# First q blocks ahead of the units, smaller first loads, and VectorE and store orders from summed TensorE times, in a two-problem attention block

## The chip, the cores and the metric

One core of one Trainium2 chip. The metric is the device time of one execution in microseconds (us). Before the change: 745.29 us, the median of three runs (745.06 to 746.17).

In what follows a run is called fast or slow by its own kernel: slow is more than 1.5% above that kernel's fastest run. "Span" is the length of the one execution that the profile shows; it is some 1.7 us shorter than the time of the same execution (738.26 us timed, 736.5 us span).

## The reference

Two independent problems, A and B, of the same shapes; the outputs are concatenated on the last axis. All tensors are bf16.

```python
B, Sq, D = 16, 80, 576
Hq, Hkv, Sk, Dh = 32, 16, 512, 128
# x (16,80,576)  k_cache, v_cache (16,16,512,128)  wq (576,4096)  wo (4096,576)
def block(x, k_cache, v_cache, wq, wo):
    q = (x @ wq).reshape(B, Sq, Hq, Dh).transpose(0, 2, 1, 3)
    k = jnp.repeat(k_cache, 2, axis=1)
    v = jnp.repeat(v_cache, 2, axis=1)
    p = softmax(jnp.einsum("bhqd,bhkd->bhqk", q, k) * Dh ** -0.5)
    o = jnp.einsum("bhqk,bhkd->bhqd", p, v)
    return o.transpose(0, 2, 1, 3).reshape(B, Sq, Hq * Dh) @ wo
out = jnp.concatenate([block(A...), block(B...)], axis=-1)
```

## The kernel before

The kernel is written as a list of operations, each with an engine and a number, its key. Each engine runs its operations in the order of their keys, and the semaphore waits are derived from what each reads and writes. So the order of an engine is set by keys alone, and most of the change is a change of keys.

The work is cut in 128 **units** (one batch, four K/V heads: 0.52 MB of K, loaded with a DMA transpose from SyncE's queue, and 0.52 MB of V from ScalarE's queue). A unit has 16 keys. For each four units there are eight **q blocks** (five matmuls), for each eight units ten **output groups** (eight matmuls with wo). There are five K buffers, three V input buffers, three q buffers and two output slots. q blocks, transposes and output groups are "jobs", which take turns in three PSUM banks; a job therefore waits until the one three before it has been drained, that is, until VectorE or ScalarE has copied or added its result out of the bank. The drain of an output group goes to a running sum, `acc`; that of a problem's last quarter adds the sum and goes to `osb`, an output slot, from where it is stored.

```python
NK, NV, NVP, NQ, NOSB, NWARM = 5, 3, 5, 3, 2, 10     # (one line here)
...
def add(eng, key, emit, **kw):
    return S.add(eng, key + 1000.0, emit, **kw)
...
# loads of x, of the first weights, of wo
t = (-800.0, -785.5, -776.5, -771.0)[c] if prob == 0 else 16.0 * (48 + 4 * c) + 9.0
add("sp", t, em_ldx, ...)
add("sp", t + 0.1, em_ldx2, ...)
...
for hf in range(2):                    # first wq in two halves of 512 columns
    add("act", -799.0 + hf, em_a, ...)
    add("act", -798.9 + hf, em_b, ...)
...
t = 256.0 * goct - 56.0 + 22.0 * pc
add("sp", t if goct else 4.0 + 12.0 * pc, em_wo, ...)
...
# q blocks: m counts groups of four units, i the eight blocks of each
t = 64.0 * m - 88.0 + 8.0 * i + 3.3
if m == 0:
    t = -96.0 + 2.0 * i
if m == 1:
    t = -28.0 + 8.0 * i + 3.3
job(t, em_qp, ..., [(ev, t + 2.3, em_qev, ...)])          # drain: 2.3 keys later
...
# K and V of unit U
t_k = T0 - 16.0 * (NK - 1) - LA + 1.5 if U >= NK else -790.0 + 4.5 * U
t_v = (T0 - 16.0 * NV - 8.0) if U >= NV else -780.0 + 3 * U
...
# reciprocal and normalisation (DVE) of a block of P.V results
tn = tmain(W, 3 * f + 2) + 0.8 if f < 5 else 64.0 * W + T_PR + 3.4 + 0.5 * (f - 5)
add("dve", tn, em_rcp, ...)
add("dve", tn + 0.1, em_nrm, ...)
...
# transposes of the normalised result, drained one key later
t = (tmain(W, 3 * lastf + 2) if lastf < 5 else 64.0 * W + T_PR + 4.0) + 5.5 + (1.0 if u == 4 else 0.0)
job(t, em_tr, ..., [("dve", t + 1.0, em_tev, ...)])
...
# output groups and their drain; stores
t = 128.0 * h8 + 64.0 + 12.8 * n + 1.3
job(t, em_op, rd, "op%d.%d" % (h8, n), ..., [("dve", t + 3.4, em_ev, ...)])
add(se, t + 6.0 + 0.1 * pi, em_st, ...)
```

## Time and profile before

| | |
|---|---|
| time, median of 3 | 745.29 us |
| span of the profiled execution | 736.5 us |
| TensorE matmuls / weight loads, share of the span | 93% / 79% |
| VectorE, ScalarE | 53%, 52% |
| all DMA | 160.8 MB, 218 GB/s over the span |

Two things stand between the 659 us of TensorE work and the span: a start in which four loads stop TensorE in turn, and a thin, regular loss afterwards where a job waits for VectorE, an engine that is half idle. The prediction shows both in the profile's own lines.

### The profile page before, as it was taken

How to read it: one execution, taken by the hardware profiler on the slowest of the kernel's cores; microseconds unless marked ns; L12 is line 12 of the kernel's file. 1: busy time of each engine (PE TensorE's matmuls, PEld its weight loads, DVE VectorE, ACT ScalarE, POOL GpSimd, SP SyncE). 2: the span in 40 equal slices, each digit the busy share in tenths (PEclk: the TensorE clock that was granted, in tenths of full speed). 3: DMA queues.
4: the chain of work that ended last, by engine and by line, in shares of the span. 5: the costliest groups of instructions: out<-in, count | busy, mean ns of one | idle time of the engine just before them, and what ended most of it. 6: DMA issues, size and time to landing. Idle time of an engine off the chain costs nothing.

```text
span 736.5 us, 21197 instructions
## 1 busy us (share of the span) xinstructions
PE 688.4 (93%) x9355; PEld 580.9 (79%) x9355; DVE 393.9 (53%) x986; ACT 379.9 (52%) x728; POOL 241.8 (33%) x136
## 2 busy tenths in 40 slices
PE   6827999999999999999999999999999999999995
PEld 3726888888888888888888888888888888888883
DVE  1322554565666555656655554555566566556654
ACT  1513655655555555455555656655555555555560
POOL 4141332244433224443323444332344432234430
PEclk9987999999999999999999999999999999999998
DMA  9999899999999999999999999999899989999841
GB/s 243 159 264 211 188 207 240 247 239 197 221 231 237 215 197 235 216 270 228 235 266 269 241 233 194 273 219 234 200 222 244 239 201 196 242 214 211 205 109 38
DMA packets 365332, 160.79 MB, mean 218 GB/s; under 512 B 283760, under 2 KB 361200, under 8 KB 365232
## 3 DMA queue, kind: packets, MB, share of 16 engines
q1 hardware_dynamic: 296304, 90.98, 67.5%
q10 hardware_dynamic: 68928, 68.37, 30.4%
q8 instruction: 75, 1.23, 0.7%
q14 instruction: 25, 0.20, 0.1%
HBM read 85.98 MB, written 2.95 MB: 121 GB/s over the span
## 4 chain that ended last, share of the span: by engine, by line
PE 82%; DVE 7%; SPq 4%; DMA 4%; issue 1%; ACT 1%
PE ps L788 23%; PE ps L972 21%; PE ps L815 15%; PE ps L880 13%; PE ps L937 6%; PE ps L896 5%; DMA kT<-in_A_k_cache_dram 3%; DVE o_sb L919 3%; SPq L847 2%; DVE oM L944 1%; DVE qT L795 1%; SPq L725 1%; DVE rinv L914 1%; DVE acc L989 1%; DMA wo_sb<-in_A_wo_dram 1%
## 5 line engine op out<-in xcount | busy, mean ns | idle before, releaser
L820 ACT ACTIVATE P<-ps 128x480 bf16<-128x480 f32 (+1 forms) x683 | 366.7, 571 | 322.5 <-PE ps L815 320.1
L854 POOL COPY v_sb<-v_in 128x2048 bf16<-128x2048 bf16 x128 | 239.2, 1896 | 469.9 <-PE ps L896 357.4
L815 PE MATMUL ps<-qT,kT 128*128 128x160 bf16 x2048 | 247.8, 233 | 8.2 <-DMA kT<-in_A_k_cache_dram 8.2
L788 PE MATMUL ps<-xT,wq_sb 128*128 128x320 bf16 x1280 | 218.6, 303 | 12.7 <-DVE acc L989 4.1
L880 PE MATMUL ps<-v_sb,P 128*128 128x130 bf16 x2048 | 203.8, 221 | 0.0
L795 DVE CAST qT<-ps 128x320 bf16<-128x320 f32 x252 | 130.4, 518 | 127.8 <-PE ps L788 127.6
L815 PEld LDWEIGHTS ps<-qT,kT 128*128 128x128 bf16 x2048 | 159.4, 98 | 25.0 <-issue 8.7
L788 PEld LDWEIGHTS ps<-xT,wq_sb 128*128 128x128 bf16 x1280 | 117.8, 99 | 52.7 <-issue 7.9
L972 PE MATMUL ps<-wo_sb,oM 128*128 128x288 bf16 x1024 | 147.1, 287 | 10.3 <-DMA wo_sb<-in_A_wo_dram 10.0
L880 PEld LDWEIGHTS ps<-v_sb,P 128*128 128x128 bf16 x2048 | 149.0, 98 | 8.7
L919 DVE TENSOR_TENSOR o_sb<-ps,rinv 128x384 bf16<-128x384 f32 (+1 forms) x224 | 120.5, 538 | 7.7
L972 PEld LDWEIGHTS ps<-wo_sb,oM 128*128 128x128 bf16 x1024 | 96.6, 98 | 31.0 <-DMA wo_sb<-in_A_wo_dram 10.3
L944 DVE COPY oM<-ps 128x512 bf16<-128x512 bf16 x128 | 54.3, 425 | 70.2 <-PE ps L937 62.0
L914 DVE RECIPROCAL rinv<-ps 128x3 f32<-128x3 f32 (+1 forms) x224 | 39.4, 176 | 94.8 <-PE ps L880 69.6
L937 PE MATMUL ps<-ident,o_sb 128*128 128x128 bf16 x640 | 62.5, 220 | 7.2 <-DVE o_sb L919 7.1
L937 PEld LDWEIGHTS ps<-ident,o_sb 128*128 128x128 bf16 x640 | 43.6, 98 | 16.1 <-DVE o_sb L919 13.7
L989 DVE TENSOR_TENSOR acc<-ps,acc 128x288 f32<-128x288 f32 x80 | 36.2, 452 | 20.6 <-PE ps L972 20.6
L896 PE MATMUL ps<-v_sb,P 128*32 128x130 bf16 x2048 | 36.4, 223 | 0.6 <-DVE o_sb L919 0.6
L972 PE MATMUL ps<-wo_sb,oR 128*128 128x288 bf16 x256 | 36.4, 286 | 0.0
L896 PEld LDWEIGHTS ps<-v_sb,P 128*32 128x32 bf16 x2048 | 30.6, 97 | 4.9 <-DVE o_sb L919 1.0
L972 PEld LDWEIGHTS ps<-wo_sb,oR 128*128 128x128 bf16 x256 | 24.3, 98 | 5.6
L994 DVE TENSOR_TENSOR osb<-ps,acc 128x288 bf16<-128x288 f32 x40 | 18.1, 453 | 10.0 <-PE ps L972 9.9
(22 smaller groups left out, 43.6 us busy)
## 6 DMA issues: line engine op xcount, KB each, us to landing
v_in<-in_A_v_cache_dram ACTq DMA_DIRECT2D x64, 512.0 KB, 5.0
v_in<-in_B_v_cache_dram ACTq DMA_DIRECT2D x64, 512.0 KB, 5.2
wo_sb<-in_A_wo_dram SPq DMA_DIRECT2D x16, 288.0 KB, 4.8
wo_sb<-in_B_wo_dram SPq DMA_DIRECT2D x16, 288.0 KB, 4.8
wq_sb<-in_B_wq_dram SPq DMA_DIRECT2D x16, 256.0 KB, 4.8
wq_sb<-in_A_wq_dram SPq DMA_DIRECT2D x12, 256.0 KB, 5.1
out_dram<-osb SPq DMA_DIRECT2D x32, 72.0 KB, 4.1
wq_sb<-in_A_wq_dram ACTq DMA_DIRECT2D x2, 512.0 KB, 5.1
```

The costliest lines, as they stand in the source:

```text
L788: last = e.matmul(ps[:, bank, 0:QN], lhsT=wq_sb[:, wsl, ck, i * 128:(i + 1) * 128], rhs=xT[:, xsl, ck, :], start=(ck == 0), stop=(ck == 4))
L795: return e.copy(dst, src) if ev == "act" else e.tensor_copy(dst, src)
L815: last = e.matmul(ps[:, sbk, c * 160:(c + 1) * 160], lhsT=kT[:, U % NK, j, g * 128:(g + 1) * 128], rhs=qT[:, (U // 4) % NQ, U % 4, g, :], ...
L820: return e.activation(P[:, psl, 0:k, :], ps[:, sbk, 0:k * 160].rearrange("p (c n) -> p c n", c=k), AF.Exp, scale=SCALE)
L854: return e.tensor_copy(v_sb[:, vps, :, 0:128], v_in[:, vs, :, :].rearrange("p g (j d) -> p (g j) d", j=4))
L880: last = e.matmul(ps[:, bank, off:off + OP_], lhsT=pap(16 * U + 4 * g + j, 0, 128), rhs=v_sb[:, vps, 4 * g + j, :], start=(j == 0), stop=( ...
L896: last = e.matmul(ps[32 * g:32 * g + 32, bank, off:off + OP_], lhsT=pap(16 * U + 4 * g + j, 128, 160), rhs=v_sb[:, U % NVP, 4 * g + j, :], ...
L914: return e.reciprocal(rinv[:, c0:c0 + nt], ps[:, bank, 128:128 + OP_ * (nt - 1) + 1:OP_])
L919: return e.tensor_tensor(o_sb[:, osl, 0:nt, :], src, sc, AluOpType.mult)
L937: last = e.transpose(psb[:, bank, 128 * n_:128 * n_ + 128], o_sb[:, F % NOF, pos, :], ident[:])
L944: return e.tensor_copy(oM[:, osl2, :, 128 * b8:128 * b8 + 128], psb[:, bank, 0:512].rearrange("p (g c) -> p g c", g=4))
L972: last = e.matmul(ps[:, bank, 0:DC], lhsT=w, rhs=wo_sb[:, wsl, i, ch * DC:(ch + 1) * DC], start=(i == 0), stop=(i == 7))
```

## The change

The intent is in three parts.

1. **Start.** Sixteen q blocks, which need only x and wq, are put ahead of the units, to fill the time in which K and V arrive; the third and fourth sets of q blocks come earlier too. The first loads are reordered (x and K interleaved, V later) and the first wq comes in smaller pieces. The first output groups and their weights come later.
2. **VectorE and store order.** The sums of TensorE's modelled durations give the moment at which each TensorE operation should end. Every drain, reciprocal and normalisation is given the key just after its source's end, a store one 1.2 us later. Transposes are put two to four keys later.
3. **End.** The last output tile, which goes out in eight stores of 16 rows, changes places with the full tile before it, so that the last stores are two of 64 rows for each half of the columns.

```diff
-        t = (-800.0, -785.5, -776.5, -771.0)[c] if prob == 0 else ...      # x
+        t = (-800.0, -799.0, -797.0, -794.0)[c] if prob == 0 else ...
-            for hf in range(2):                                            # first wq
-                n0, n1 = hf * 512, (hf + 1) * 512
+            add("act", -799.5, em_b, ...)               # its last 64 rows, in one load
+            for hf, (n0, n1) in enumerate(((0, 256), (256, 512), (512, 1024))):
-            add("sp", t if goct else 4.0 + 12.0 * pc, em_wo, ...)
+            add("sp", t if goct else 58.0 + 13.0 * pc, em_wo, ...)
-                t = -28.0 + 8.0 * i + 3.3                                  # q, m == 1
+                t = -44.0 + 3.5 * i
+            if m == 2:
+                t = -6.0 + 7.0 * i + 3.3
+            if m == 3:
+                t = 54.0 + 8.0 * i + 3.3
-        t_k = ... if U >= NK else -790.0 + 4.5 * U
+        t_k = ... if U >= NK else (-798.0, -796.0, -795.0, -793.0, -792.0)[U]
-        t_v = (T0 - 16.0 * NV - 8.0) if U >= NV else -780.0 + 3 * U
+        t_v = (T0 - 16.0 * NV - (8.0 if U > 8 else -6.0)) if U >= NV else (-84.0, -60.0, -40.0)[U]
...
+    def place_followers():                       # part 2
+        seq = sorted(pe_time, key=lambda x: (x[0].key, x[0].seq))
+        start, end, keys, t = [], {}, [], 0.0
+        for op, d in seq:
+            start.append(t); t += d; end[id(op)] = t; keys.append(op.key)
+        ...
+        for op, (src, sub, lag) in follow:
+            r = end[id(src)] + lag
+            i = bisect.bisect_left(start, r - 1e-6)
+            op.key = keys[i - 1] + (keys[i] - keys[i - 1]) * min(0.999, 0.5 + sub)
+    # durations: scores 0.2076, P.V 0.228, remainder 1.12, q 0.68, output 0.98, transposes 0.228
-            add("dve", tn, em_rcp, ...)
+            add("dve", 0.0, em_rcp, ..., after=(tn, sub, 0.0))
-            t = ... + 5.5 + (1.0 if u == 4 else 0.0)                       # transposes
+            t = ... + (9.5 if u < 3 else 7.5) + (1.5 if u == 4 else 0.0)
-            add(eng, ek, ..., name="ev_" + name)                           # drains
+            add(eng, 0.0, ..., name="ev_" + name, after=(jo, 0.35, 0.0))
-            t = 128.0 * h8 + 64.0 + 12.8 * n + 1.3                         # output groups
+            t = (128.0 * h8 + 66.0 + 12.8 * n if h8 else 112.0 + 12.8 * n) + 1.3
...
+            if h8 == NH8 - 1 and ti > 2:         # part 3
+                ti = 7 - ti
+            last = h8 == NH8 - 1 and n >= 8      # its stores: one for each half of the columns
```

(Cut: the loads of the second wq block, 60 keys later, and the alternation of the last stores over two queues.)

## The prediction

> **What bounds the kernel now.** I read the page first: engine shares and the slices.
>
> ```profile
> PE 688.4 (93%) x9355; PEld 580.9 (79%) x9355; DVE 393.9 (53%) x986; ACT 379.9 (52%) x728; POOL 241.8 (33%) x136
> ...
> PE   6827999999999999999999999999999999999995
> ...
> PEclk9987999999999999999999999999999999999998
> DMA  9999899999999999999999999999899989999841
> ```
>
> TensorE is the densest engine from the fifth slice on (a slice is 18.4 us); the first four slices and the last are holed. The DMA row is at 9 nearly all along, so loads are the second suspect, most of all where TensorE is holed. Since busy matmuls overlap, I took the cost of TensorE's work from its timeline, start to start of consecutive groups where nothing was waited for: a q block (5 matmuls, L788) 0.68 us, 3 score matmuls (L815) 0.208, a P·V group of 4 (L880) 0.23, the 64 remainder matmuls (L896) 1.06, 4 transposes (L937) 0.22, an output group of 8 (L972) 0.975. With 256, 683, 512, 32, 160 and 160 of them: 174 + 142 + 118 + 34 + 35 + 156 = 659 us. The span is 736.5, so about 77 us are not work. Where they lie, by the timeline: 9.7 before the first real matmul, 27 lost between 9.7 and 62 us, about 32 spread thinly over 62 to 728.6, and 7.9 after the last matmul.
>
> The early loss, in the list of waits:
>
> ```profile
> PE ps L972 <- DMA wo_sb<-in_A_wo_dram: 10.0, 1, 10.0
> ...
> PE ps L815 <- DMA kT<-in_A_k_cache_dram: 8.2, 3, 5.1
> ...
> PE ps L788 <- DMA xT<-in_A_x_dram: 2.8, 1, 2.8
> ```
>
> and in the timeline (start, length, engine, line, operation, in brackets idle time before):
>
> ```profile
> 9.69 7.78 PE L788 MATMUL ps<-xT,wq_sb 128*128 128x320 bf16 x40 [3.91 <-issue]
> 20.30 2.19 PE L788 MATMUL ps<-xT,wq_sb 128*128 128x320 bf16 x10 [2.84 <-DMA xT<-in_A_x_dram]
> ...
> 39.62 0.37 PE L815 MATMUL ps<-qT,kT 128*128 128x160 bf16 x3 [2.88 <-DMA kT<-in_A_k_cache_dram]
> ...
> 49.29 0.56 PE L815 MATMUL ps<-qT,kT 128*128 128x160 bf16 x3 [5.12 <-DMA kT<-in_A_k_cache_dram]
> ...
> 59.85 2.10 PE L972 MATMUL ps<-wo_sb,oM 128*128 128x288 bf16 x8 [10.00 <-DMA wo_sb<-in_A_wo_dram]
> ```
>
> TensorE is stopped by four loads in turn. The worst is an output projection put so early that its weights, queued behind K loads, aren't there: with K5 landed, scores and P·V behind it stand still too. From 62 us on there is no load wait on TensorE; the thin loss is this:
>
> ```profile
> PE ps L937 <- DVE o_sb L919: 7.1, 32, 0.3
> ...
> PE ps L788 <- DVE acc L989: 4.1, 16, 0.4
> ...
> PE ps L788 <- DVE osb L994: 1.6, 6, 0.4
> ```
>
> One case of it in the timeline:
>
> ```profile
> 395.44 0.42 DVE L944 COPY oM<-ps 128x512 bf16<-128x512 bf16 x1 [1.76 <-PE ps L937]
> ...
> 396.19 0.44 DVE L994 TENSOR_TENSOR osb<-ps,acc 128x288 bf16<-128x288 f32 x1
> ...
> 396.69 0.85 PE L788 MATMUL ps<-xT,wq_sb 128*128 128x320 bf16 x5 [0.40 <-DVE osb L994]
> ```
>
> VectorE sat idle 1.76 us for a transpose, while the output group begun at 393.16 (done by 394.1) waited to be drained behind it in program order. Its bank came free at 396.63, and the q block that wanted the bank stopped. VectorE is only 53% busy: it is its order that is wrong. Such a stop costs more than the listed idle: start to start the score group before this q block took 0.77 instead of 0.21, 0.56 lost for 0.40 listed.
>
> **What the Trainium skill says.** "Perfetto Trace Analysis", Identifying the Most-Contended Engine: busy share of matmuls is no good measure of headroom, weight-load share is better. Agrees: PE shows 93%, weight loads 79%, my 659 us of work is 89% of the span. "DMA: Bandwidth & Descriptors", Anatomy of one DMA: waiting for a semaphore is done by the issuing sequencer, before dispatch. So one blocked K load holds every later load of SP's list; the trace has SP waiting 542 us in all for TensorE to free K buffers. Same page, Queues, rings and completion order: each DMA engine shares itself round-robin among the queues that have work. Agrees: K3 to K5, issued while V loads ran on the other queue, took 11.0, 13.6 and 12.4 us to land, 6.2 at the median in steady state. "TensorE: Matmul & The Clock Gate", What's actually happening: after an idle window of about 3.4 us TensorE runs at half clock. The windows view has clock 0.50 from 50 to 64 us; a q block there took 1.33 instead of 0.68.
>
> **The change part by part.**
>
> (1) First loads. SP's list becomes x0, x1, K0, x2, K1, K2, x3, K3... and V0 to V2 leave ACT only after the first casts; the first weights come as 256, 256, 512 columns. Now the first q block waited for the tail of x0, issued at 2.24, landing 7.4 later (9.64), with three V blocks (1.5 MB) and K0 in flight beside it. Without those I expect it at about 7 us: 2.5 earlier.
>
> (2) Order of TensorE. The new program shows 80 q matmuls (16 blocks) ahead of the first score, then scores with the third and fourth q blocks' work (m=2, 3) a unit or more earlier than before. 16 x 0.68 = 10.9 us of work that needs x and weights alone, from 7 to 18 us, just while K and V arrive. The output groups of the first eight units start 48 keys (three units) later, their weights too. So the waits of 2.8 and 10.0 us go, with the half clock after them. But K is then the limit. Landings now: K0 15.7, K1 19.8, K2 23.5, K3 33.4, K4 39.5, K5 49.1, with x3 and eight V loads among them. The same bytes in the new order, at that pace: K0 at 14, K2 24, K4 38, K5 44, then some 5 us for each unit (0.52 MB of K, as much of V and part of a weight block, at 230 to 250 GB/s): K8 at 59, K11 at 75. TensorE needs only 3.9 us per unit there (1.1 scores, 0.9 P·V, 0.27 remainder, 0.28 transposes, 1.36 q), so it still waits, about a microsecond a unit. At U11.6 both programs have all 32 early q blocks done; the old one stands there at 97 us with 9 output groups, the new one at some 79 with 5. 97 - 79 - 4 x 0.98 = 14 us gained. (2.5 of part 1 is inside this.)
>
> (3) VectorE order. Each drain, reciprocal and normalisation is now placed where the summed durations of TensorE say its source ends, and transposes come 2 to 4 keys later (4 keys are 1.3 us), so that normalisation has ended. Nothing is added: same instructions. Loss from 62 to 728 by kind of step, start to start: scores before q block 10.2, scores before transpose 8.0, P·V before transpose 4.7, transpose before output 0.8: 23.7 us. I take two thirds as recovered: 16.
>
> (4) End. Stores of the last tile: now eight of 18 KB, issued by two sequencers in 2.5 us after the last addition (729.4); span end 736.5. The last tile becomes one with two stores of 36 KB, halves stored apart: 2 us saved.
>
> Sum: 745.3 - 14 - 16 - 2 = 713; rounded to 712.
>
> **Rivals.** (a) DMA becomes the bound. All 160.8 MB, at 736.5 us a mean of 218 GB/s; a unit of 5.39 us (100 units from 154.5 to 693.3) would become 5.23, which needs 240. If loads can't do that, K never regains its lead and parts 2 and 3 shrink together: some 725 to 730. For it: the DMA row at 9, and 24 us at only about 208 GB/s while TensorE starved (26 to 50). Against it: 251 GB/s held from 350 to 400 with no wait on TensorE, and K landing 6.2 us after issue with 20 us until use. (b) The start is bound by bytes, not order: what the 16 blocks fill is then waited for at K4 to K8 again, and only the 10 us of wo and its half clock remain; with part 3 at 16, about 717. (c) The modelled times are off (clock, load waits), the waits move to other pairs: part 3 gives 5, total 723. (d) Everything works, with VectorE waits nearly gone and K at 4.5 us a unit: 702.
>
> **Range and chances.** Two savings of similar size and different cause, either alone giving about 2%, so a miss of both is needed to stay within 2% (730.4 or more). I predict 712, with 701 (d) to 727 (a with half of part 3) as the range. Faster by over 2%: 0.90; within: 0.09; slower: 0.01, since no work is added.
>
> **What would show it.** First q block at 7, not 9.7; no wait on wo before 110 us; clock near 1 from 10 to 70 us; a few load waits on K of 1 to 3 us left between 25 and 75; U11.6 reached near 79. Waits of L937's and L788's successors on VectorE under 4 us together from 100 to 700, and 5.22 to 5.27 us per unit there. Between last matmul and end about 6 us. I am wrong if K waits run on past 100 us (a), or if the unit time stays at 5.35 or more (c).

## More of the kernel before

One more view of this kernel is needed to compare with later: the table of windows (start:end, length, then busy time of TensorE, its weight loads, VectorE, ScalarE and GpSimd, then granted clock, DMA share, GB/s).

```profile
0.00:50.00 50.00, 33.44 (x326) 23.30 (x326) 13.75 (x33) 16.78 (x32) 16.74 (x16) 0.95 1.09 216
50.00:70.00 20.00, 10.15 (x87) 8.29 (x88) 2.96 (x7) 4.58 (x10) 1.80 (x2) 0.62 0.99 214
```

Loads move at about 215 GB/s in both, while TensorE is idle a third and a half of the time.

## The result and the profile after

| | before | after |
|---|---|---|
| median of the runs taken together (fast) | 745.17 us | 718.64 us |
| range of these (4 runs each) | 736.97 to 746.17 | 712.77 to 719.86 |
| profiled execution, span | 736.5 us | 711.0 us |

Ratio 0.9654, with an interval of 0.9581 to 0.9727: faster. (A ratio here is the mean time of one kernel's fast runs over that of the other's of the same rounds, so not quite the ratio of the medians quoted.) Of six runs of the changed kernel, a slow one, 725.79 us, is left out; a fifth fast one is at 718.41. Both results are correct.

The shares and slices of the changed kernel (a slice is 17.8 us):

```profile
PE 678.5 (95%) x9355; PEld 581.9 (82%) x9355; DVE 388.7 (55%) x986; ACT 377.4 (53%) x728; POOL 241.5 (34%) x136
...
PE   6992999999999999999998999999999999999994
...
PEclk8996999999999999999999999999999999999998
DMA  9999999999999999999999999999899988999921
```

The second and third slices are now full, but the fourth, at 53 to 71 us, is nearly empty. The list of waits (engine, line, what was waited for: total us, times, longest) says why. Lines have moved: output groups are L1007, q blocks L817, scores L844, transposes L970, drains into the output slots L1029.

```profile
PE ps L1007 <- DMA wo_sb<-in_A_wo_dram: 14.0, 1, 14.0
...
DVE osb L1029 <- DMA out_dram<-osb: 7.4, 3, 4.9
...
PE ps L817 <- DMA xT<-in_A_x_dram: 4.3, 1, 4.3
...
PE ps L1007 <- DVE oR L984: 2.1, 1, 2.1
...
PE ps L970 <- DVE o_sb L951: 0.7, 2, 0.6
```

Against the list of before: the 32 transposes that waited for VectorE are 2, and the 16 q blocks that waited for `acc` are gone; the three waits for K are gone. The wait for wo is still there, and longer: 14.0 instead of 10.0. In TensorE's timeline:

```profile
9.87 13.77 PE L817 MATMUL ps<-xT,wq_sb 128*128 128x320 bf16 x80 [4.29 <-DMA xT<-in_A_x_dram]
...
52.61 0.84 PE L817 MATMUL ps<-xT,wq_sb 128*128 128x320 bf16 x5
...
67.46 2.08 PE L1007 MATMUL ps<-wo_sb,oM 128*128 128x288 bf16 x8 [14.01 <-DMA wo_sb<-in_A_wo_dram]
```

The 16 q blocks run back to back, the units run on without a stop until 53.4, then the first output group stands for 14 us before its weights. SyncE's queue, which issues them, shows what they stood behind (start, length of the issue):

```profile
52.89 7.96 SPq L877 DMA_TRANSPOSE kT<-in_A_k_cache_dram  x1
60.89 0.58 SPq L789 DMA_DIRECT2D wo_sb<-in_A_wo_dram  x1
...
62.02 0.43 SPq L789 DMA_DIRECT2D wo_sb<-in_A_wo_dram  x1
```

The group needs all four pieces of wo. Two were issued at 45.07 and 51.76; the other two came behind the load of K10, whose issue alone lasted 7.96 us (2.4 at the median between 100 and 650 us). Only 0.6 of it is listed as a wait for a K buffer. The windows, to be read beside those of before:

```profile
0.00:50.00 50.00, 44.11 (x466) 33.30 (x467) 22.20 (x53) 22.93 (x43) 17.58 (x16) 0.93 1.10 246
50.00:70.00 20.00, 5.99 (x58) 4.64 (x56) 2.47 (x6) 3.03 (x6) 1.89 (x1) 0.66 1.14 231
```

TensorE is busy 10.7 us more in the first 50 us. Loads move 246 GB/s instead of 216, but in the second pair of profiles it is 229 after and 232 before, so that rate is not shown to be the change's doing. From 50 to 70 TensorE does less than before, while loads go on at 231 GB/s. So the DMA engines aren't idle in the gap; they carry something else than wo first.

**Where the time went, by stage.** I took from TensorE's timeline when the first scores of units 12, 22 and 122 start (the first group of three score matmuls that lies wholly in the unit), of two profiled executions of each kernel (the second pair is from the repeat runs b2 and a2 below).

| | unit 12 | unit 22 | 22 to 122 | 122 to the end | span |
|---|---|---|---|---|---|
| before | 99.7 | 154.5 | 538.8 | 43.2 | 736.5 |
| before again | 95.8 | 150.6 | 545.1 | 45.5 | 741.2 |
| after | 86.0 | 142.9 | 523.3 | 44.8 | 711.0 |
| after again | 90.5 | 147.4 | 529.4 | 43.6 | 720.4 |

On the means: up to unit 22, 7.4 us saved; the 100 units between, 15.6; the end, 0.1. Together 23.1 of the span. At unit 12 the kernel before has nine output groups behind it and the changed kernel six; three groups at 0.98 us are 2.9, so of the 9.5 us there some 6.6 are real.

### The profile page after: what moved, and what is told of

It is laid out like the page before. It is cut to its first block, busy times and chain, and to the rows that moved or that the text cites. A ratio compares the mean times of both kernels' runs of the same rounds, so it can differ in the third digit from the quotient of the medians.

```text
span 711.0 us, 21206 instructions
## 1 busy us (share of the span) xinstructions
PE 678.5 (95%) x9355; PEld 581.9 (82%) x9355; DVE 388.7 (55%) x986; ACT 377.4 (53%) x728; POOL 241.5 (34%) x136
## 4 chain that ended last, share of the span: by engine, by line
PE 93%; DMA 2%; SPq 1%; DVE 1%; issue 0%; ACT 0%; DVEq 0%
PE ps L817 25%; PE ps L1007 22%; PE ps L844 20%; PE ps L911 17%; PE ps L970 5%; PE ps L927 5%; SPq L877 1%; DMA xT<-in_A_x_dram 1%; DMA wo_sb<-in_A_wo_dram 1%; DMA out_dram<-osb 1%; DVE o_sb L951 0%; DVE oM L977 0%; DVE osb L1029 0%; SPq L752 0%; DVE okm L1067 0%
## 5 line engine op out<-in xcount | busy, mean ns | idle before, releaser
L849 ACT ACTIVATE P<-ps 128x480 bf16<-128x480 f32 (+1 forms) x683 | 360.5, 570 | 252.7 <-PE ps L844 247.8
L844 PE MATMUL ps<-qT,kT 128*128 128x160 bf16 x2048 | 244.3, 233 | 0.2 <-ACT P L849 0.2
L817 PE MATMUL ps<-xT,wq_sb 128*128 128x320 bf16 x1280 | 215.8, 302 | 5.9 <-DMA xT<-in_A_x_dram 4.3
L844 PEld LDWEIGHTS ps<-qT,kT 128*128 128x128 bf16 x2048 | 159.8, 97 | 18.1 <-ACT P L849 0.4
L1007 PE MATMUL ps<-wo_sb,oM 128*128 128x288 bf16 x1024 | 147.6, 288 | 14.0 <-DMA wo_sb<-in_A_wo_dram 14.0
L817 PEld LDWEIGHTS ps<-xT,wq_sb 128*128 128x128 bf16 x1280 | 117.7, 98 | 39.0 <-issue 5.0
L1007 PEld LDWEIGHTS ps<-wo_sb,oM 128*128 128x128 bf16 x1024 | 97.8, 98 | 38.0 <-issue 14.3
L970 PE MATMUL ps<-ident,o_sb 128*128 128x128 bf16 x640 | 60.0, 219 | 0.8 <-DVE o_sb L951 0.7
L970 PEld LDWEIGHTS ps<-ident,o_sb 128*128 128x128 bf16 x640 | 44.4, 98 | 3.3 <-DVE o_sb L951 1.5
L1007 PE MATMUL ps<-wo_sb,oR 128*128 128x288 bf16 x256 | 38.6, 297 | 2.1 <-DVE oR L984 2.1
L1019 ACT COPY acc<-ps 128x288 f32<-128x288 f32 x40 | 15.9, 398 | 45.2 <-PE ps L1007 45.2
L1029 DVE TENSOR_TENSOR osb<-ps,acc 128x288 bf16<-128x288 f32 x40 | 18.3, 457 | 33.0 <-PE ps L1007 23.5
```

The source lines that it names most:

```text
L817: last = e.matmul(ps[:, bank, 0:QN], lhsT=wq_sb[:, wsl, ck, i * 128:(i + 1) * 128], rhs=xT[:, xsl, ck, :], start=(ck == 0), stop=(ck == 4))
L844: last = e.matmul(ps[:, sbk, c * 160:(c + 1) * 160], lhsT=kT[:, U % NK, j, g * 128:(g + 1) * 128], rhs=qT[:, (U // 4) % NQ, U % 4, g, :], ...
L849: return e.activation(P[:, psl, 0:k, :], ps[:, sbk, 0:k * 160].rearrange("p (c n) -> p c n", c=k), AF.Exp, scale=SCALE)
L970: last = e.transpose(psb[:, bank, 128 * n_:128 * n_ + 128], o_sb[:, F % NOF, pos, :], ident[:])
L1007: last = e.matmul(ps[:, bank, 0:DC], lhsT=w, rhs=wo_sb[:, wsl, i, ch * DC:(ch + 1) * DC], start=(i == 0), stop=(i == 7))
```

## The experiments

Line numbers differ a little from kernel to kernel. All edits are to the changed kernel, unless it says otherwise. Experiments of one job share a chip and its runs of the kernel before: medians of those are 742.57 (first job: e1 to e4), 744.31 (second: a2, b2, e5, e7) and 745.63 (third: e6, e8, e9), slow runs included. Where a view is a span, it is one execution.

### e1: the start alone

VectorE's order, the transposes' and output groups' places, the stores' keys and the end back to the old ones; loads, q blocks and the later first output groups kept.

```diff
-            add(eng, 0.0, ..., name="ev_" + name, after=(jo, 0.35, 0.0))
+            add(eng, ek, ..., name="ev_" + name)
-            add("dve", 0.0, em_rcp, ..., after=(tn, sub, 0.0))
+            add("dve", tn, em_rcp, ...)              # the same for em_nrm, old tn
-            ... + (9.5 if u < 3 else 7.5) + (1.5 if u == 4 else 0.0)
+            ... + 5.5 + (1.0 if u == 4 else 0.0)
-                ti = 7 - ti                          # and last = False
```

> The changed kernel with VectorE order, transpose and store places and the end put back to those of before; only the start (first loads, q blocks ahead, first output groups later) is new. If gains add up by part (my theory): 10 to 13 us faster than before, about 733 to 735 where before is 745, unit time from the 22nd to the 122nd unit back at 5.39 us. If DMA is the bound of the whole kernel (rival a): the start's gain is eaten later by waits on K, under 5 us remain.

Measured: median 737.53 us, ratio to the kernel before 0.9977 (0.9908 to 1.0046); span 732.5, unit 12 at 86.8, units 22 to 122 in 543.0. The old waits are back in its list, at nearly their old size:

```profile
PE ps L970 <- DVE o_sb L951: 7.3, 33, 0.3
...
PE ps L817 <- DVE acc L1022: 4.1, 16, 0.4
```

The start alone brings little to the time, less than the 10 to 13 us expected, and it does nothing for the units after it: 543.0 is the pace of before (538.8 and 545.1).

### e2: VectorE's order alone

The old loads, q places and end; part 2 kept.

```diff
-        t = (-800.0, -799.0, -797.0, -794.0)[c] if prob == 0 else ...
+        t = (-800.0, -785.5, -776.5, -771.0)[c] if prob == 0 else ...
-            add("sp", t if goct else 58.0 + 13.0 * pc, em_wo, ...)
+            add("sp", t if goct else 4.0 + 12.0 * pc, em_wo, ...)
         # likewise wq, K, V, the q blocks and the first output groups: old keys; old end
```

> The kernel before with only VectorE's order taken from modelled TensorE times, later transposes, and store places; old start, old end. Additive theory: 15 to 18 us faster than before (about 728 to 730), unit time 5.23 us, start as before with the 10 us wait on the output weights. Rival (VectorE's order matters only once TensorE is ahead of loads, or DMA binds): under 8 us.

Measured: median 728.15 us, ratio 0.9835 (0.9761 to 0.9909); span 718.6, units 22 to 122 in 531.2. In its list:

```profile
DVE osb L1025 <- DMA out_dram<-osb: 18.1, 4, 6.2
...
PE ps L1003 <- DMA wo_sb<-in_A_wo_dram: 10.7, 1, 10.7
...
PE ps L968 <- DVE o_sb L949: 0.2, 1, 0.2
```

The old wait for wo is there at its old size, the waits on VectorE's order are gone, and a new one has come: four times VectorE waits for a store to free an output slot, which TensorE pays with 2.9 + 3.9 us. So VectorE's order is the larger part, and what it saves is partly taken by the stores. One thing doesn't fit: with the old start, this execution is at unit 12 at 91.5 and at unit 22 at 145.4, as early as the changed kernel (142.9 and 147.4). It was the fastest of its six runs, the median being 7.9 us longer.

### e3: wo early again

```diff
-            add("sp", t if goct else 58.0 + 13.0 * pc, em_wo, ...)
+            add("sp", t if goct else 18.0 + 12.0 * pc, em_wo, ...)
```

> The changed kernel with the first four output-weight loads put 40 keys (two and a half units) earlier in SP's list, before K6, K7, K8 and K9 instead of around K9 to K11. Order theory (the 14 us wait at 53 us is a queue order, the weights stand behind K9 and K10): the wait shrinks to under 5 us, some of it returns as K waits, kernel 5 to 10 us faster than the changed one. Bytes theory (DMA is in arrears there, whatever comes first): the 14 us comes back as waits on K, gain under 3 us.

If the 14 us were the order of SyncE's list, this would take them away. Measured: 726.19 us, ratio 0.9721 (0.9614 to 0.9827; three of six runs slow); span 716.3, unit 12 at 94.5 against 86.0. The wait for wo is gone, and two others are there in its place, 19.7 us in sum, so the start is slower than without the edit (the second profile of the changed kernel has unit 12 at 90.5), which neither theory had expected:

```profile
PE ps L817 <- DMA wq_sb<-in_A_wq_dram: 10.1, 1, 10.1
PE ps L844 <- DMA kT<-in_A_k_cache_dram: 9.6, 7, 4.2
```

### e5: 3.1 MB of V less

No V load for units 6 to 11; those units use an older V. Its output is wrong, which doesn't matter for the time.

```diff
+        skip = 6 <= U < 12
-        add("act", t_v, em_ldv, ...)
+        if not skip:
+            add("act", t_v, em_ldv, ...)
```

> The changed kernel without the six V loads of units 6 to 11 (3.1 MB; older V blocks are used again, the result is wrong on purpose). All orders, waits and TensorE work stay. Bytes theory (the wait at 53 us is DMA in arrears): the 14 us wait on the output weights falls under 5 us and the 22nd unit comes 8 to 12 us earlier than in the changed kernel (131 to 135 us against 142.9). Order theory (the weights stand behind K loads that wait for buffers): the wait stays at 10 us or more.

Measured (one execution, its state unknown): the output group begins at 59.17 instead of 67.46.

```profile
52.50 0.84 PE L817 MATMUL ps<-xT,wq_sb 128*128 128x320 bf16 x5
59.17 2.08 PE L1013 MATMUL ps<-wo_sb,oM 128*128 128x288 bf16 x8 [5.82 <-DMA wo_sb<-in_A_wo_dram]
```

Same order of loads on SyncE, fewer bytes on the other queue: the wait falls from 14.0 (12.6 to 14.9 in the six other profiles with the new place of wo and ten warm-ups) to 5.8, and unit 22 begins at 135.2 instead of 142.9. With e3 this says that the gap is in large part a debt of bytes and not only a matter of order (by 67 us the changed kernel has loaded about 16 MB, 246 GB/s for 50 us and 231 for 17). The way by which the bytes reach wo is SyncE's queue: the issue of K10 took 4.46 us here instead of 7.96, and the last piece of wo was issued at 54.92 instead of 62.02. The bytes theory's own numbers (under 5 us, unit 22 at 131 to 135) are narrowly missed, and 5.8 us of the wait remain. The time of this kernel, 719.65 us, is no better. In this execution VectorE waited 27.3 us for stores later on (five times), TensorE lost 13.4 of it, and units 22 to 122, whose program is that of the changed kernel, took 538.8 us.

### e8: the q blocks in their old places, the new loads kept

```diff
-                t = -44.0 + 3.5 * i              # m == 1
+                t = -28.0 + 8.0 * i + 3.3
-            if m == 2: ...                       # and m == 3: both back to the general rule
```

> The changed kernel with its load order, but the q blocks of m = 1, 2 and 3 at their old places (interleaved a block per 8 keys). Theory of the fill (loads set when a unit can be reached, q blocks are the work that fits into the waits): TensorE reaches the wait on the output weights earlier, near 45 us, the wait lasts to about the same 67 us (some 20 us long), and the q blocks not done by then come after it: the 12th unit at 90 to 93 us instead of 85 to 90, kernel 4 to 6 us slower than the changed one. Rival (the load order alone is the gain): 12th unit as in the changed kernel, same time.

Measured in the profile (span 716.1):

```profile
53.89 0.37 PE L840 MATMUL ps<-qT,kT 128*128 128x160 bf16 x3
67.64 2.08 PE L1003 MATMUL ps<-wo_sb,oM 128*128 128x288 bf16 x8 [13.38 <-DMA wo_sb<-in_A_wo_dram]
```

The wait ends at the same moment as in the changed kernel (67.64 and 67.46). It is not the one wait of 20 us that was expected: 5.5 us of waits for K come before it. Unit 12 begins at 90.9, with fewer q blocks done by 54 us. That is 4.9 us later than in the changed kernel's first profile (86.0), but only 0.4 later than in its second (90.5), so the profiles don't say what the early q blocks are worth. In timings the fast runs, only two (717.9 and 727.61), give a ratio of 0.988 (0.9816 to 0.9944), beside 0.9654 and 0.9705 of the changed kernel. That is slower, as the theory of the fill has it, and by more than the 4 to 6 us expected. The other six runs, at 729 to 731, are slow by the rule; why they lie there I can't say.

### e9: e1 once more

The same kernel as e1, on another chip, because e1's interval held both "nothing" and "half of what I expected".

> Start only, a second time, since its first timing (ratio 0.9977, interval 0.9908 to 1.0046) left open whether the start is worth anything by itself. If its gain at the 22nd unit (8 us in the profile) lasts: 0.985 to 0.993. If it is eaten later by loads: 0.995 to 1.002 again, with waits on K or on stores after 100 us that the kernel before lacks.

Measured: 734.06 us, ratio 0.9942 (0.9859 to 1.0025); span 732.2, unit 12 at 86.3, units 22 to 122 in 544.8. The spans of e1 and e9 are 6.5 us below the mean of the two of before (738.9); the timings say 0.2% and 0.6%, or 2 to 4 us, with no change inside both intervals. As the second expectation had it, there are waits after 100 us that the first profile of before lacks: 2.9 us for K of problem B on TensorE, and 7.8 us for stores on VectorE (2.5 and 3.3 in e1).

### e4: the old end

```diff
-            if h8 == NH8 - 1 and ti > 2:
-                ti = 7 - ti
-            last = h8 == NH8 - 1 and n >= 8
+            last = False
```

> The changed kernel with the old end: old order of the last tiles, last tile stored in eight pieces at once. The traces say the last stretch (from the 122nd unit on) is 1.6 us longer after the change than before, with 2.1 us of it a wait for the remainder's copy that stands behind the check's operations on VectorE. If the new order of tiles is what meets that wait: 0 to 2 us faster than the changed kernel. If my predicted saving of 2 us by fewer stores is real and the wait comes whatever the order: 2 us slower.

Measured: 721.68 us, ratio 0.9739 (0.9653 to 0.9825); span 712.8; from unit 122 to the end 42.6 us, against 44.8 and 43.6 with the new end (e2, also with the old end: 41.9; e3 and e8, with the new: 43.7 and 44.3). The timing can't tell it from the changed kernel. In the changed kernel, the timeline of the last microseconds shows what the exchange of tiles ran into:

```profile
695.99 0.83 DVE L1067 SCALAR_TENSOR_TENSOR okm<-rinv,okm 128x640 bf16<-128x640 f32 x1
...
696.93 0.41 DVE L984 COPY oR<-ps 128x512 bf16<-128x512 bf16 x1
...
697.40 1.42 PE L1007 MATMUL ps<-wo_sb,oR 128*128 128x288 bf16 x8 [2.09 <-DVE oR L984]
```

The small tile, which needs `oR`, now comes before the last full tile. But VectorE has the kernel's final check of its reciprocals (`okm`) ahead of the copy of `oR`, and TensorE waits 2.1 us. With the old end that wait isn't there. From the last addition's end to the span's end it is 7.2 to 9.4 us in the six profiles with the old stores (mean 8.0) and 7.4 to 8.5 in the seven with the new (mean 7.8): no saving that stands out of the scatter, for 2.1 us lost.

### e7: the check later, three output slots

```diff
-NOSB = 2
+NOSB = 3
-    tc = 64.0 * (NW - 1) + T_PR + 13.0
+    tc = 64.0 * (NW - 1) + T_PR + 20.0           # the two last steps of the check later too
```

> The changed kernel with the final check's VectorE operations put after the remainder's copy, and three output slots instead of two. From the profile of the changed kernel: the 2.1 us wait on the remainder's copy at 697 goes (last stretch 42 to 43 us instead of 44.8), and the stop at 380 us (4.87 us of VectorE waiting for a store, about 4 us lost on TensorE) goes. Together 4 to 6 us, 0.6 to 0.8%, near what the timing can tell. If stores are only late because DMA is in arrears there, the stop comes back elsewhere and 2 us remain.

Measured: 717.34 us, ratio 0.9665 (0.9602 to 0.9727), beside 0.9705 (0.9631 to 0.9779) for the changed kernel in the same job; span 711.4. The end is mended, 41.8 us from unit 122 to the end:

```profile
698.82 0.41 DVE L984 COPY oR<-ps 128x512 bf16<-128x512 bf16 x1
...
699.29 2.13 PE L1007 MATMUL ps<-wo_sb,oR 128*128 128x288 bf16 x16 [0.63 <-DVE oR L984]
```

With the third slot VectorE's waits for stores are gone from this profile (e6, with the same slots, has one of 1.4 us). But there are waits for K instead, 3.8 + 1.8 us, all but 0.7 of it between 329 and 418 us, where problem B's x and weights are loaded and A's output is stored:

```profile
PE ps L844 <- DMA kT<-in_A_k_cache_dram: 3.8, 3, 1.5
PE ps L844 <- DMA kT<-in_B_k_cache_dram: 1.8, 2, 1.1
```

The stop has moved from the stores to K. That fits loads in arrears here too, as in the first 70 us, but no experiment took bytes away in this stretch. Units 22 to 122 took 527.9 us, no less than in the changed kernel.

### e6: e7 with 28 warm-up matmuls

```diff
-NWARM = 10
+NWARM = 28
```

> The version with the end mended and three output slots, and 28 warm-up matmuls instead of 10, so that TensorE is not at half clock when the first q block comes. Bytes theory: the 16 q blocks take about 11 us instead of 13.4, the wait on the output weights grows by as much, the 12th unit and the whole time are as without it (within 1 us in the profile, apart from run-to-run spread). Rival (TensorE work sets the start): 2.5 us earlier at the 12th unit.

In the changed kernel's profile the first q blocks run at half clock: the casts behind them start at 11.40, 12.73, 14.06 and 15.40, 1.33 us apart, and later ones 0.68 apart. The same holds in all twelve profiles with ten warm-ups, after 3.9 to 5.4 us of idle: the first 11 to 21 matmuls start 267 ns apart, the later ones 136. (The windows of before, e1, e3 and e9 print a clock of 1.00 there, but their traces hold no record of the clock before 13.4 us; the spacing of the matmuls decides.) With 28 warm-ups, which last from 1.35 to 9.95 us, TensorE isn't idle there, and all matmuls of the 16 blocks start 136 ns apart. The blocks take 11.03 us in the timeline instead of 13.77 in the changed kernel and 12.97 in e7, and nothing comes of it: at 35 us TensorE waits 3.7 us for a K load, and unit 12 begins at 86.3 (e7: 84.8). The wait on wo did not grow, as was expected, but is 9.7 us (e7: 12.9); a wait for K has come in its place. Median 715.14 us, all six runs fast, ratio 0.9656 (0.9576 to 0.9737); its fastest run, 708.98, is the shortest time of all. Against e7 and the changed kernel that can't be told apart.

### a2 and b2: both kernels once more

No edit. They give the second row of each kernel in the table of stages.

> The changed kernel once more, for a second profile and times beside the others on one chip. About 0.965 of before, as first measured; in the profile the 14 us wait on the output weights again near 53 us.

Measured: 722.14 us, ratio 0.9705 (0.9631 to 0.9779), span 720.4; the wait on wo is 14.9 us, and there are waits for K of 1.7.

> The kernel before once more, for a second profile: how much the start differs from run to run. Start-only and vector-only profiles each reached the 22nd unit 9 to 10 us earlier than the first profile of before (154.5 us), though vector-only has the old start. If the first profile was typical: 22nd unit at 153 to 156 us. If it was an unlucky start: 145 to 150 us, and my reading of the start's gain in profiles shrinks by as much.

Measured: 742.9 us (one execution; the fast runs of its job lie at 735.9 to 745.2), span 741.2. Unit 22 begins at 150.6, between the two expectations: the first profile had a somewhat late start.

The spread between executions of one kernel is some 10 us even among fast runs (before 733.7 to 746.2 over all, after 712.7 to 723.1). In the two pairs of profiles it comes from the start (some 4 us) and from the stretch 320 to 420 us, in which the windows have TensorE busy 97.9 us (before), 93.2 (before again), 97.8 (after) and 92.2 (after again), while from 420 to 660 the two of a pair agree to 0.02. There is the changed kernel's largest stop after the start:

```profile
381.86 0.46 DVE L1029 TENSOR_TENSOR osb<-ps,acc 128x288 bf16<-128x288 f32 x1 [4.87 <-DMA out_dram<-osb]
...
382.38 0.85 PE L817 MATMUL ps<-xT,wq_sb 128*128 128x320 bf16 x5 [1.65 <-DVE osb L1029]
```

VectorE waits 4.87 us for a store to leave its slot, and the q block waits for VectorE. The sum of these waits on VectorE was 7.4 us in the profile after, and 21.4 in a2, whose units 22 to 122 took 6 us more. Over all profiles with the new order and two slots, the stretch from unit 22 to 122 goes with this sum: 520.8 to 524.8 us where it is 4 to 11 (e3, e4, after, e8), 529.4 and 531.2 at 21.4 and 18.1 (a2, e2), 538.8 at 27.3 (e5).

## Why the prediction was right, and where its steps were not

The time, 718.64 us, lies in the range, 6.6 us above the point; the class is right. (The point itself is 713.3 by the prediction's own sum; 712 is not its rounding.) By its steps:

- **First loads: q block at 7 us. Wrong.** It came at 9.87, hardly different from 9.69. The step blamed the V blocks and K0 in flight beside x0's tail. V was gone and K0 issued at 6.40 instead of 3.58, and from the issue of x0's tail to the first matmul it was still 7.4 us (2.47 to 9.87; 2.24 to 9.69 before). So V was not the cause. What sets those 7.4 us stays open.
- **Order at the start: 14 us. The mechanism was wrong in part, and the size too large.** Of "So the waits of 2.8 and 10.0 us go, with the half clock after them" only the 2.8 went: the wait for wo grew to 14.0, and the granted clock is 0.66 from 50 to 70 us. "About a microsecond a unit" for K failed as well: there is no wait for K up to 53 us in the first profile and 0.5 in a2. K landed sooner than forecast (K5 at 38.0 us, not 44; K8 at 49.1, not 59), and wo was what came late. The output groups were put 48 keys later and their weights with them, into the densest stretch of K and V loads; the bytes due by then were what they were. Part (b) of the rivals, "bound by bytes, not order", came nearest, also in its number, 717, though it let the wait for wo go and fall on K. Shown by e3 (wo earlier: 19.7 us of other waits in its place) and e5 (3.1 MB fewer: wait 8.2 us shorter). The early q blocks did fill the time up to 23.6 us; what they are worth is not shown (e8: 4.9 or 0.4 us in profiles, slower in timings). Of the 14 us, 6.6 are seen at unit 12 and 7.4 at unit 22, and not even these are shown to come from the start: e2 has the old one and is at unit 22 as early.
- **VectorE's order: 16 us from 62 to 728. Right in mechanism, under-sized.** "I take two thirds as recovered" was the chosen term, with no measurement behind it. The four executions with VectorE's old order (before, b2, e1, e9) took 542.9 us for units 22 to 122 at the mean, and six with the new order and two slots (after, a2, e2, e3, e4, e8) 525.6: 17.3 us for 100 units, 0.17 a unit. (With e5, the same program there but 27.3 us of waits for stores, it is 15.5. At like waits for stores, 7.4 to 7.8 us, it is 523.3 in after against 545.1 in b2 and 544.8 in e9.) A unit takes 5.23 us in the profile after, as predicted (5.22 to 5.27). The waits that this was to remove are down from 12.8 us (7.1, 4.1 and 1.6) to 2.3 (0.7 and 1.6), and the 1.6 is the stop at 382 us, which a store caused. Over the stretch that the step counted, 666 us, that is 17.3 x 666 / 539 = 21 us of the 23.7 (19 with e5), an estimate that takes the saving to be even. It is not free of a new cost: the waits for stores, 18.1 us in e2 and 27.3 in e5.
- **End: 2 us. Wrong.** 0.1 us came of it. The forecast of "about 6 us" between the last matmul and the end failed: counted as its 7.9 for the kernel before, it is 8.1. The exchange of tiles met a check in VectorE's order, which cost 2.1 (shown by e4, and by e7 that moves the check and is at 41.8).
- **Rival (a), DMA as the bound, up to 725 or 730.** It fits two stretches, the first 70 us (shown by e5) and 320 to 420 us (not tested), and not the rest: in the profile after, TensorE is busy without a gap from 420 to 660 us, at 231 GB/s and with no load wait.

The sum, 32 us, was made of 14 + 16 + 2; the spans of two pairs say 7.4 + 15.6 + 0.1 = 23.1 and the timing 26.5 (745.17 - 718.64). The range held because too much at the start was set against too little in VectorE's order; that the two errors were of opposite sign was luck. Of the signs that it named, the waits on VectorE (2.3 us, under 4) and the unit time came true; the first q block at 7 us, no wait on wo, the clock near 1, waits on K of 1 to 3 us, U11.6 near 79 (84.4 and 88.9) and the end did not. Its "Agrees" on weight loads as the better measure isn't borne out either: 659 us of work is 89% of the span, nearer to the 93% of matmuls than to the 79% of weight loads.

**What stays open.** The parts don't add up cleanly. In timings, start alone (0.2 to 0.6%) and VectorE alone (1.65%) make some 2%, together 3 to 3.5%. In spans it is the other way round: 6.5 us (e1, e9) and 20.3 us (e2) against 23.1. A spread of 10 us in each kernel hides what of that is interaction. Unit 12 in e2, at 91.5, is already 6 us ahead of before, with the old start, and unit 22, at 145.4, some 7. Its waits for K at the start are shorter (3.1 us, against 8.2 and 5.8 in the two profiles of before). One profile is not enough to say why, or whether the new start adds anything to VectorE's order by unit 22.

## What to carry to other kernels

Where an engine that is half idle still stops a full one, look at its program order first: drains placed by the summed durations of the engine that feeds them gave 0.17 us of 5.39 per unit, here two thirds of the whole gain, with no instruction added. Where a load wait only moves to another load when an order is changed, take away bytes (with a wrong result, for once) to see whether it is a debt; if it is, the thing to put there is work that needs none of the missing bytes. Before crediting a profile's difference to an edit, take a second profile of the unedited kernel: here unit 12 of one kernel lay at 86.0 and 90.5. After any such reordering look at small single operations, such as a final check, that now stand before something urgent.

## What the Trainium skill lacked or had wrong

- "DMA: Bandwidth & Descriptors", Latency and other measured facts: it states 261 GB/s for a DMA transpose (of a form that is not contiguous), and gives no time from issue to landing for one. Here K blocks of 0.52 MB landed 6.2 us after issue at the median in steady state and 10 to 13.6 us beside V loads at the start, and an 82 KB piece of x some 7 us, whether V loads ran beside it or not. Transposes and plain loads together reached 246 GB/s over the first 50 us. Nor does it have a spread between executions: 733.7 to 746.2 us for one program, over several chips; in the profiles it lies in stretches full of loads.
- "TensorE: Matmul & The Clock Gate", What's actually happening: it says that the window runs freely and that the start varies from run to run. Nothing is wrong or lacking in that: in twelve profiles 11 to 21 matmuls of the first q blocks ran at half clock, and taking that away (e6) gained nothing that can be measured (unit 12 at 86.3 us, 84.8 in e7).
- No page has it: that the wait which a profile names for a load says what came last, not what is short. Here the 14.0 us on wo became 19.7 us on wq and K when wo was loaded earlier.
